# Fused attention and two-layer kernel: first weight chunks unpacked in PSUM, keys of units 0 to 3 by TensorE transposes, low half of g on VectorE in 16 steps

## The chip, the cores and the metric

The kernel runs on one core of a Trainium2 chip. The metric is device time in microseconds (us); lower is better. Engines: TensorE (PE, its weight loads PEld), VectorE (DVE), ScalarE (ACT), GpSimd (POOL), and SyncE (SP), which issues the DMAs.

## The reference, cut

```python
# attention with decay: 4 batches, 8 heads, 768 tokens, head size 48
for t in range(S):
    y[:, :, t] = einsum('bhd,bhde->bhe', r_t, state + (u * k_t) v_t)
    state = w * state + k_t v_t
x = y as (3072, 384)
# first layer: 384 -> 2048 -> 384
h = x @ w_in
g = h if h >= 1, 0 if h <= -1, else (h + 1)**2 / 4
x1 = g @ w_out
# second layer: each token goes to its best of 8 experts
out = gate * (relu(x1 @ w1[e]) @ w2[e])
```

All tensors are float32. `w_in` and `w_out` arrive as 64-bit numbers.

## The kernel before

Every float32 product is made of three matmuls in a rounded format (`prod3`, lines 293 to 295): high by high, high by low, low by high. So every operand is split into a high half (a ScalarE copy) and a low half (operand minus high half).

**Attention** works on 24 units of 128 tokens, six per batch. For a unit: the transposed r and k are scaled by powers of w (`prep_rk`, VectorE); `s0_pe` multiplies them into two 128x512 products in PSUM, which VectorE masks (`s0_ev`); `s2_pe` adds the unit's keys times values to the state; `s1_pe` makes the transposed output y; `s3_hi` and `s3_lo` split it into `xh` and `xl`. The keys in natural layout (`kk`) are loaded apart and scaled on GpSimd (`prep_kk`). The diagonal term with u is a product on GpSimd (`prep_dv`) that TensorE adds to y by transposes in the first 8 units (`DIAG`); later it is written into the masked product by predicated copies on VectorE (`s0_dg`). The states of units 0 to 4 of the first batch go through an identity matmul (`by_pe`).

**Weights** of the first layer come in 16 chunks of 768 64-bit numbers per partition (`w_load`). Three VectorE passes (`w_bits`, lines 361, 364, 367) put each number's bits together as a float32 in a scratch tile, ScalarE copies the high half (`w_hi`, line 382), GpSimd subtracts (`w_lo`, line 386).

**The first layer** runs in 96 steps, each one block of 512 tokens and 128 of the 2048 columns. A step is 9 matmuls into a bank of tag `h` (two banks), three ScalarE passes into a tile `a` (lines 677, 681, 684), a max on VectorE (line 687), the high half `gh` on ScalarE (line 691), the low half `gl` on GpSimd (line 696), and 9 matmuls into three accumulator banks. The first 14 steps cover columns of blocks 0 and 1. **The second layer** follows with the weights of the expert that token 0 chose; the branch for other experts does not run here.

**The order** of all this is written out by a planner (`Schedule`) when the kernel is built: each task has an engine, a price (`COST`), a due time (shifted by `SHIFT`), the tasks it waits for, and the buffers it takes. The planner fills each engine's list; on the chip each engine works through its list in order and waits for semaphores. Buffers that matter: four `ld` tiles (attention tiles and weight chunks), two `x1` tiles, three PSUM banks `att`, two `h`, three accumulators. `SP` issues loads in the planned order and waits for a free tile. Before the first output matmul, gaps that the planner sees on TensorE are filled with matmuls that do nothing (`keep_warm`, line 602).

Of the kernel before, what the change touches and what calls it, by code (L numbers as in the profile page):

```python
# [33 lines left out]
DIAG = 8  # L34
# [23 lines left out]
class Schedule:  # L58
# [5 lines left out]
    LOCK = {"rk", "wb1", "wb2", "wb3", "dd", "x2l", "w2lo", "slo"}  # L64
# [150 lines left out]
SHIFT = {"dd": -118.5, "dg": -152.25, "dg2": 85, "dp": -121, "dv": 7, "e0": 37.75, "e0c": -69.5, "e0l": 11.25, "e1":  # L215
# [3 lines left out]
         5.75, "max": -5, "mixl": 6, "o": 18.5, "o2": -773.75, "oh": -43.5, "ost": -52.5, "over": 99.75,  # L219
# [30 lines left out]
def fused_kernel(ctx, tc, att, wcol, wrow, ub, ucol, win, wout, emb, tau, w1, w2, out):  # L250
# [268 lines left out]
    def by_pe(u):  # L519
        return u < UPB - 1  # L520
# [165 lines left out]
    def m1_max(a, hp):  # L686
        nc.vector.tensor_tensor(out=a, in0=hp, in1=a, op=ALU.max)  # L687
# [356 lines left out]
    first = {n: i - 100 for i, n in enumerate("a0 w0 n0 ub b0 a1 n1 b1 w1".split())}  # L1044
# [6 lines left out]
    for u in range(NU):  # L1051
# [13 lines left out]
        l2 = add("l2", f"u{u}", "SP", 1.1, lambda u=u: att_load(u, "n"), due=first.get(f"n{u}", due - 9 - 2), alloc=[nb])  # L1065
        rk = add("rk", f"u{u}", "DVE", 1.57, lambda u=u: prep_rk(u), [l0], due - 8, use=[ab])
        kk = add("kk", f"u{u}", "Pool", 1.3, lambda u=u: prep_kk(u), [l2, wkc], due - 6, alloc=[kkb], use=[nb])
        if u < RAMP:
# [3 lines left out]
            dg = add("dg", f"u{u}", "ACT", 0.2, lambda u=u: dg_ev(u), [dp], due - 5.4, alloc=[dgb], use=[dpb])  # L1072
# [4 lines left out]
        if u < DIAG:  # L1077
# [39 lines left out]
    for ci, c in enumerate([x for f in range(NF // 2) for x in (("in", f), ("out", f))]):  # L1117
# [443 lines left out]
```

## Time and profile before

| | |
|---|---|
| median of 3 runs | 739.37 us (738.45 to 743.44) |
| profiled execution | 740.02 us, span 738.1 us |
| TensorE busy | 721.9 us (98%), 4977 matmuls |
| VectorE, ScalarE, GpSimd busy | 381.7, 394.0, 280.1 us |
| DMA | 73.45 MB |

The span runs from the first to the last instruction. An engine is busy while an instruction of its own executes; TensorE's filler matmuls count as busy.

### The profile page before, as it was taken

To read this page: it belongs to the slowest core of one execution; us is meant where nothing else is said; L and a number is where in the kernel's file an instruction comes from. 1 tells how busy PE (TensorE), PEld (TensorE's weight loads), DVE (VectorE), ACT (ScalarE), POOL (GpSimd) and SP (SyncE) were. 2 spreads that over 40 slices of the span, in tenths; PEclk is the share of its full clock that TensorE was granted. 3 is DMA by queue.
4 is the path that set the end of the run, shared out by engine and by line. 5 is a ranking of instruction groups with operands and counts; after the bars stand their busy time and mean duration, and the time that the engine had idled before them with its cause. 6 is when DMAs were issued, how large, how long until landed. Compare 5 with 4: busy or idle time off the path is not lost.

```text
span 738.1 us, 12336 instructions
## 1 busy us (share of the span) xinstructions
PE 721.9 (98%) x4977; PEld 596.5 (81%) x4977; DVE 381.7 (52%) x606; ACT 394.0 (53%) x700; POOL 280.1 (38%) x225
## 2 busy tenths in 40 slices
PE   8899999999999999999999999999999999999995
PEld 6777887777888877887888888887989898879994
DVE  7789799787871363367455452132233324142342
ACT  2365758654656377566775676666243324252343
POOL 6899986845535254234423142333010100100000
PEclk9999999999999999999999999999999999999999
DMA  7746444434330253134353142001111202001100
GB/s 265 271 170 238 148 170 138 137 126 130 134 136 1 66 185 130 40 132 149 129 170 129 44 130 85 1 0 44 44 43 44 86 1 85 11 12 44 65 22 27
DMA packets 24724, 73.45 MB, mean 100 GB/s; under 512 B 2377, under 2 KB 8658, under 8 KB 24658
## 3 DMA queue, kind: packets, MB, share of 16 engines
q1 hardware_dynamic: 24658, 72.57, 29.3%
q8 instruction: 41, 0.67, 0.4%
q14 instruction: 25, 0.20, 0.1%
HBM read 61.56 MB, written 11.01 MB: 98 GB/s over the span
## 4 chain that ended last, share of the span: by engine, by line
PE 87%; DVE 4%; DMA 4%; ACT 2%; issue 1%; POOL 0%; SPq 0%; ACTq 0%; POOLq 0%; DVEq 0%
PE psh L293 13%; PE psh L294 12%; PE psh L295 12%; PE acc L293 9%; PE acc L294 9%; PE acc L295 9%; PE o L295 5%; PE o L293 4%; PE o L294 4%; PE psy L535 4%; DMA att<-att 3%; PE psa L502 3%; PE pskv L564 1%; DMA w<-win 1%; DVE sc L367 1%
## 5 line engine op out<-in xcount | busy, mean ns | idle before, releaser
L696 POOL TENSOR_TENSOR gl<-a,gh 128x512 fp32r<-128x512 f32 x96 | 137.9, 1447 | 183.8 <-ACT gh L691 180.0
L687 DVE TENSOR_TENSOR a<-psh,a 128x512 f32<-128x512 f32 x96 | 66.1, 689 | 134.8 <-ACT a L684 126.2
L293 PE MATMUL psh<-xh,win_h 128*128 128x512 f32 x288 | 115.9, 402 | 1.0 <-DVE a L687 0.9
L293 PE MATMUL acc<-gh,wout_h 128*128 128x512 f32 x288 | 114.8, 399 | 0.0
L294 PE MATMUL acc<-gl,wout_h 128*128 128x512 f32 x288 | 113.9, 396 | 0.0
L295 PE MATMUL acc<-gh,wout_l 128*128 128x512 f32 x288 | 113.9, 395 | 0.0
L294 PE MATMUL psh<-xl,win_h 128*128 128x512 f32 x288 | 113.8, 395 | 0.0
L295 PE MATMUL psh<-xh,win_l 128*128 128x512 f32 x288 | 113.8, 395 | 0.0
L677 ACT ACTIVATE a<-psh,half 128x512 f32<-128x512 f32 x96 | 65.7, 684 | 74.9 <-PE psh L295 60.4
L954 ACT ACTIVATE gh<-psh 128x512 fp32r<-128x512 f32 (+1 forms) x56 | 30.0, 536 | 108.7 <-PE psh L295 107.0
L959 DVE SCALAR_TENSOR_TENSOR gl<-psh,gh 128x512 fp32r<-128x512 f32 (+1 forms) x56 | 34.4, 614 | 102.8 <-ACT gh L954 102.7
L831 POOL TENSOR_TENSOR sq<-sq 128x512 f32<-128x512 f32 (+1 forms) x14 | 15.9, 1135 | 182.4 <-ACT sq L826 161.1
L691 ACT ACTIVATE gh<-a 128x512 fp32r<-128x512 f32 x96 | 59.4, 624 | 32.0 <-DVE a L687 19.2
L293 PEld LDWEIGHTS psh<-xh,win_h 128*128 128x128 f32 x288 | 54.1, 188 | 16.9 <-DVE a L687 2.3
L295 PE MATMUL o<-w2h,gl 128*128 128x384 f32 x192 | 65.0, 339 | 1.4 <-DVE gl L959 1.4
L293 PEld LDWEIGHTS acc<-gh,wout_h 128*128 128x128 f32 x288 | 54.1, 188 | 13.7 <-issue 0.4
L293 PE MATMUL o<-w2h,gh 128*128 128x384 f32 x192 | 64.8, 337 | 0.1
L295 PEld LDWEIGHTS psh<-xh,win_l 128*128 128x128 f32 x288 | 54.1, 188 | 13.1
L294 PEld LDWEIGHTS acc<-gl,wout_h 128*128 128x128 f32 x288 | 54.1, 188 | 13.0 <-POOL gl L696 0.4
L295 PEld LDWEIGHTS acc<-gh,wout_l 128*128 128x128 f32 x288 | 54.1, 188 | 13.0
L294 PE MATMUL o<-w2l,gh 128*128 128x384 f32 x192 | 64.5, 336 | 0.0
L294 PEld LDWEIGHTS psh<-xl,win_h 128*128 128x128 f32 x288 | 54.1, 188 | 12.2
(167 smaller groups left out, 1290.1 us busy)
## 6 DMA issues: line engine op xcount, KB each, us to landing
att<-att SPq DMA_DIRECT2D x22, 736.0 KB, 5.3
w<-wout SPq DMA_DIRECT2D x16, 768.0 KB, 4.2
w<-win SPq DMA_DIRECT2D x16, 768.0 KB, 4.3
attn<-att SPq DMA_DIRECT2D x20, 384.0 KB, 4.2
x1d<-x SPq DMA_DIRECT2D x6, 768.0 KB, 4.1
out<-o SPq DMA_DIRECT2D x11, 384.0 KB, 2.5
x1f<-x1d SPq DMA_DIRECT2D x5, 768.0 KB, 4.9
hw<-w SPq DMA_DIRECT2D x8, 384.0 KB, 3.8
```

The source lines that it names most:

```text
L293: nc.tensor.matmul(o, lhsT=sh, rhs=mh, start=first, stop=False, skip_group_check=True)
L294: nc.tensor.matmul(o, lhsT=sh, rhs=ml, start=False, stop=False, skip_group_check=True)
L295: nc.tensor.matmul(o, lhsT=sl, rhs=mh, start=False, stop=last, skip_group_check=True)
L502: nc.tensor.matmul(a[j][:, p, :], lhsT=s["k2"][64 * j:64 * j + 64, p, :], rhs=s["r2"][64 * j:64 * j + 64, p, :], start=True, stop=True)
L535: nc.tensor.matmul(o, lhsT=lhsT, rhs=rhs, start=q in fresh, stop=stop, skip_group_check=True)
L677: nc.scalar.activation(out=a, in_=hp, func=AF.Relu, bias=half[:, 0:1], scale=0.5)
L687: nc.vector.tensor_tensor(out=a, in0=hp, in1=a, op=ALU.max)
L691: nc.scalar.activation(out=gh, in_=a, func=AF.Copy)
L696: (eng or nc.gpsimd).tensor_tensor(out=gl, in0=a, in1=gh.bitcast(F32), op=ALU.subtract)
L831: nc.gpsimd.tensor_tensor(out=q[:, 0, :n], in0=q[:, 0, :n], in1=q[:, kk, :n], op=ALU.add)
L954: nc.scalar.activation(out=gh, in_=hp, func=AF.Relu)
L959: nc.vector.scalar_tensor_tensor(out=gl, in0=hp, scalar=0.0, in1=gh.bitcast(F32), op0=ALU.max, op1=ALU.subtract)
```

## The change

Constants choose how many units or steps take a new path.

- `KK_PE` 4: units 0 to 3 get their natural keys from `kk_pe`, four TensorE transposes of the scaled keys into a bank `att`, and `kk_ev`, a ScalarE copy. Their loads in natural layout are gone.
- `W_PSUM` 2: chunks 0 and 1 land in the two `x1` tiles. Their bits are put together in two accumulator banks (`w_pbits`), and `w_psplit` makes the high half on ScalarE and the low half on VectorE.
- `G_PSUM` 16: in steps 0 to 15 the max writes into the `h` bank; ScalarE and VectorE take the high and the low half from there. The bank is held until then, and `a` only until the max.
- `DV_PSUM` 4: in units 0 to 3 `prep_dv` runs on VectorE and reads its small factor from PSUM; the copy `dg_ev` is gone there.
- `DIAG` is 6 in place of 8, `BY_PE` is 4 in place of 5.
- The loads are asked for in the order a0, b0, a1, b1, w0, w1, `SHIFT` is another table, and the planner prices the routing steps `rt3` higher. `ON_DVE` is empty.

```diff
-DIAG = 8
+DIAG = 6
 ...
     if kind == "rt3":
-        return 0.12 if eng == "ACT" else {0.3: 0.35, 0.9: 0.95, 1.0: 1.1}[dur]
+        return 1.45 if eng == "ACT" else {0.3: 0.37, 0.9: 1.25, 1.0: 1.3}[dur]
 ...
+KK_PE, W_PSUM, G_PSUM, DV_PSUM, BY_PE = 4, 2, 16, 4, 4
 ...
     def w_load(c):
         kind, f = c
-        t = atp.tile([128, 1536], F32, tag="ld", name="w64", bufs=4).bitcast(U64)
+        if 2 * f + (kind == "out") < W_PSUM and c not in stage_t:
+            t = xp.tile([128, KD, 512], F32, tag="x1", name="w64").rearrange("p k n -> p (k n)").bitcast(U64)
+        else:
+            t = atp.tile([128, 1536], F32, tag="ld", name="w64", bufs=4).bitcast(U64)
 ...
+    def w_pbits(c, i):
+        t64 = stage_t[c]
+        hw, lw = t64[:, :, 1], t64[:, :, 0]
+        if i == 1:
+            w_buf[c] = [psum(f"acc{j + 1}", [128, 512], "psw", 1)[:, :x.stop - x.start] for j, x in w_parts(c)]
+        for j, x in w_parts(c):
+            m = w_buf[c][j].bitcast(U32)
+            if i == 1:
+                nc.vector.tensor_scalar(out=m, in0=hw[:, x], scalar1=3, scalar2=0x3FFFFFFF, op0=ALU.logical_shift_left,
+                                        op1=ALU.bitwise_and)
+            elif i == 2:
+                nc.vector.scalar_tensor_tensor(out=m, in0=hw[:, x], scalar=0xC0000000, in1=m, op0=ALU.bitwise_and,
+                                               op1=ALU.bitwise_or)
+            else:
+                nc.vector.scalar_tensor_tensor(out=m, in0=lw[:, x], scalar=29, in1=m, op0=ALU.logical_shift_right,
+                                               op1=ALU.bitwise_or)
 ...
+    def w_psplit(c, lo):
 ...
+            if lo:
+                nc.vector.tensor_tensor(out=l, in0=m, in1=h.bitcast(F32), op=ALU.subtract)
+            else:
+                nc.scalar.activation(out=h, in_=m, func=AF.Copy)
 ...
+    def kk_pe(u):
+        st[u]["kkp"] = psum("att", [128, NP, C], "pskk", 3)
+        for p in range(NP):
+            nc.tensor.transpose(st[u]["kkp"][:, p, :], st[u]["k2"][:, p, :], ident)
+
+    def kk_ev(u):
+        st[u]["kk"] = atp.tile([128, H, D], F32, tag="kk", name="kk", bufs=2)
+        nc.scalar.activation(out=st[u]["kk"].rearrange("q (p j) d -> q p j d", p=NP),
+                             in_=st[u].pop("kkp").rearrange("q p (j d) -> q p j d", j=2)[:, :, :, 0:D], func=AF.Copy)
 ...
-        dg = s["dg"].rearrange("p (a j) -> p a j", a=NP)
+        eng = nc.vector if u < DV_PSUM else elem("dv", f"u{u}")
+        dg = (s["dgp"] if u < DV_PSUM else s["dg"]).rearrange("p (a j) -> p a j", a=NP)
 ...
     def by_pe(u):
-        return u < UPB - 1
+        return u < BY_PE
 ...
-    first = {n: i - 100 for i, n in enumerate("a0 w0 n0 ub b0 a1 n1 b1 w1".split())}
+    first = {n: i - 100 for i, n in enumerate("a0 b0 a1 b1 w0 w1".split())}
 ...
-        l2 = add("l2", f"u{u}", "SP", 1.1, lambda u=u: att_load(u, "n"), due=first.get(f"n{u}", due - 9 - 2), alloc=[nb])
+        l2 = u >= KK_PE and add("l2", f"u{u}", "SP", 1.1, lambda u=u: att_load(u, "n"), due=first.get(f"n{u}", due - 9 - 2), alloc=[nb])
 ...
-        wb, sb = Buf("ld"), Buf("x1")
+        wb, sb = Buf("x1" if ci < W_PSUM else "ld"), Buf("x1")
 ...
+        gk = "h" if k < G_PSUM else "a"
+        gb = hb if k < G_PSUM else ab
+        q = add("max", f"k{k}", "DVE", 0.7, lambda k=k, gk=gk: m1_max(got["a", k], got["h", k], got[gk, k]), [q], T[k], use=[ab, hb])
+        q = add("gh", f"k{k}", "ACT", 0.65, lambda k=k, n=n, gk=gk: got.update({("gh", k): m1_gh(got[gk, k], n)}), [q], T[k], alloc=[ghb], use=[gb])
+
+        def gl(k=k, s=s, gk=gk):
+            gq[s[:3]] = got["gh", k], m1_gl(got[gk, k], got["gh", k], s[3], nc.vector if k < G_PSUM else elem("gl", f"k{k}"))
+        q = add(*(("glp", f"k{k}", "DVE") if k < G_PSUM else ("gl", f"k{k}", "Pool")), 1.45, gl, [q], T[k], alloc=[glb], use=[gb, ghb])
```

## Rows read from the trace of the kernel before

**Rows 1.** Stretches of the span: length, busy us (instructions) of each engine, clock, DMA.

```profile
0.00:7.11 7.11, 4.79 (x25) 4.49 (x25) 4.22 (x15) 1.77 (x2) 2.44 (x14) 1.00 0.59 186
7.11:38.93 31.82, 28.76 (x444) 22.60 (x444) 25.41 (x28) 9.25 (x27) 27.05 (x24) 1.00 0.83 289
38.93:160.00 121.07, 120.76 (x843) 96.66 (x840) 107.11 (x108) 80.66 (x138) 98.60 (x65) 1.00 0.49 166
...
730.82:738.10 7.28, 0.00 (x0) 0.00 (x0) 0.42 (x1) 0.45 (x2) 0.00 (x0) 0.86 0.21 66
sum 738.10, PE 721.89 PEld 596.53 DVE 381.71 ACT 394.01 POOL 280.12; mean PE 72.19 PEld 59.65 DVE 38.17 ACT 39.40 POOL 28.01
```

**Rows 2.** The same view for the filler matmuls of line 602 alone.

```profile
7.11:38.93 31.82, 4.61 (x30) 3.74 (x30) 1.00 0.83 289
38.93:160.00 121.07, 0.71 (x4) 0.52 (x4) 1.00 0.49 166
```

**Rows 3.** Chain that ended last, first 40 us: start, us, what.

```profile
by line: DMA att<-att 37.1%; PE psa L502 9.0%; PE psy L535 6.9%; DVE att L445 6.9%; issue 5.5%; DVE sc L367 4.9%; PE pskv L560 4.0%; POOL kr L464 3.2%; DVE at L510 3.0%; PE psdg L470 2.6%; ACT state L525 2.6%; PE pskv L564 2.5%; PE psy L539
...
15.73 1.20 DVE at L510 x2
16.93 1.96 DVE sc L367
...
18.90 4.73 DMA att<-att
...
28.70 6.36 DMA att<-att
...
35.15 1.24 DVE att L445
```

**Rows 4.** VectorE groups of the first 160 us: busy us, mean ns, idle before.

```profile
L687 DVE TENSOR_TENSOR a<-psh,a 128x512 f32<-128x512 f32 x25 | 17.1, 686 | 10.4 <-ACT a L684 9.8 <-POOL ru L459 0.3
...
L515 DVE COPY_PREDICATED at<-ident,dg 128x512 f32<-128x512 int32 x4 | 5.7, 1479 | 0.0
L595 DVE TENSOR_TENSOR xl<-psy,xh 128x384 fp32r<-128x384 f32 x9 | 4.9, 549 | 0.4 <-ACT xh L589 0.2
```

**Rows 5.** One line, the second unpack pass: shortest, median, longest in ns.

```profile
L364 DVE SCALAR_TENSOR_TENSOR sc<-w,sc x16: 957/1654/2526, 12.0 to 144.4; 128x768 uint32<-128x768 uint32 x16
```

**Rows 6.** TensorE in order of time: start, us, what; first 75 us.

```profile
5.85 0.66 PE L608 MATMUL pstw<-ident,pwt 128*128 128x128 f32 x4
6.34 0.39 PE L602 MATMUL wu<-mask,ident 128*128 128x128 f32 x2
...
37.59 0.91 PE L560 MATMUL pskv<-state,ident 128*128 128x384 f32 x2
38.44 0.56 PE L564 MATMUL pskv<-att,kk 128*48 128x48 f32 x16
...
62.85 0.49 PE L539 MATMUL psy<-ident,dv 128*128 128x128 f32 x3
63.27 1.08 PE L535 MATMUL psy<-at,att 128*32 128x128 f32 x32
```

**Rows 7.** GpSimd groups of the first 160 us: busy us, mean ns, idle before.

```profile
L696 POOL TENSOR_TENSOR gl<-a,gh 128x512 fp32r<-128x512 f32 x24 | 40.1, 1676 | 15.0 <-ACT gh L691 11.1 <-issue 3.6 <-PE psh L295 0.2
L386 POOL TENSOR_TENSOR win_l<-sc,win_h 128x768 fp32r<-128x768 f32 x8 | 16.4, 2053 | 3.8 <-ACT win_h L382 3.7
```

**Rows 8.** Waits of TensorE: total us, times, longest.

```profile
PE o L295 <- DVE gl L959: 1.4, 2, 0.7
```

**Rows 9.** All engines in order of time, 82.3 to 89 us.

```profile
82.33 0.39 PE L293 MATMUL psh<-xh,win_h 128*128 128x512 f32 x1
...
86.08 0.63 ACT L684 ACTIVATE a<-a 128x512 f32<-128x512 f32 x1
...
86.82 0.69 DVE L687 TENSOR_TENSOR a<-psh,a 128x512 f32<-128x512 f32 x1 [3.30 <-ACT a L684]
...
88.63 0.40 PE L293 MATMUL psh<-xh,win_h 128*128 128x512 f32 x1
```

More of the change, by code (lines that the diff above doesn't have):

```diff
@@ L63 @@
             "PE": {"ACT": 0.24, "DVE": 0.2, "Pool": 0.25}, "Pool": {"ACT": 0.09, "DVE": 0.09, "PE": 0.12}}
-    LOCK = {"rk", "wb1", "wb2", "wb3", "dd", "x2l", "w2lo", "slo"}
+    LOCK = {"rk", "wb1", "wb2", "wb3", "dd", "x2l", "w2lo", "slo", "krv", "kkv", "dvv", "ru0v", "ru1v", "wlov", "glv"}
     MAIN = {"h", "o", "h2", "o2", "rt0"}
@@ L72, in add @@
         due += self.shift.get(kind, 0) + self.shift.get(item, 0)
+        if eng == "Pool" and (kind, item) in ON_DVE:
+            kind, eng = kind + "v", "DVE"
         t = Task(kind, item, eng, cost(kind, item, eng, dur), fn, deps, due, list(alloc), list(use) + list(alloc), list(after))
@@ L171 @@
         "t5a": 0.12, "tw": 0.85, "dp": 0.84, "t4": 0.2, "pe0": 0.2, "pe1": 0.25, "le1": 0.1, "fl1": 0.1, "rt2": 0.2,
[1 row of a table removed]
+        "s0": 0.89, "krv": 0.605, "kkv": 0.475, "dvv": 0.55, "ru0v": 0.475, "ru1v": 0.475, "wlov": 0.87, "glv": 0.605,
+        "kkt": 0.5, "kkc": 0.42, "dvp": 0.6, "wp1": 0.6, "wp2": 0.93, "wp3": 0.93, "whp": 0.8, "wlp": 0.93, "glp": 0.605}
 COST_256 = {"x2h": 0.33, "sqa": 0.33, "shi": 0.33, "x2l": 0.34, "slo": 0.34, "gl2": 0.34, "gh2": 0.31, "rt1": 0.31,
@@ L212, in d_pe @@
     return n / 2300 + 0.011
-SHIFT = {"dd": -118.5, "dg": -152.25, "dg2": 85, "dp": -121, "dv": 7, "e0": 37.75, "e0c": -69.5, "e0l": 11.25, "e1":
[3 rows of a table removed]
-         5.75, "max": -5, "mixl": 6, "o": 18.5, "o2": -773.75, "oh": -43.5, "ost": -52.5, "over": 99.75,
[26 rows of a table removed]
+SHIFT = {"": 368.5, "b0": 11, "b1": 72.75, "b2": 141.5, "b3": -2.5, "b4": -265.5, "b5": -0.25, "b6": 172.25, "dd":
[28 rows of a table added]
+         "whi": -44.75, "whp": 130, "wkc": 32.5, "wl": 7.75, "wlo": -99.25, "wlp": -90.5, "wp1": -36, "wp2": 14.75,
+         "wp3": 40.5, "x1ld": -15.75, "x1st": -1, "x2l": -19.25, "x2ld": -68}
 U_DVE, U_PE, W_DVE = 4.7, 3.5, 4.0
+ON_DVE = {}
+KK_PE, W_PSUM, G_PSUM, DV_PSUM, BY_PE = 4, 2, 16, 4, 4
 @with_exitstack
@@ L369, in w_bits, with w_parts @@
             del stage_t[c]
+    def w_parts(c):
+        n = 256 if c[0] == "in" else 384
+        return [(0, slice(0, n)), (1, slice(n, 768))]
+    def w_pbits(c, i):
[14 more added lines that the diff above has]
+                                               op1=ALU.bitwise_or)
+        if i == 3:
+            del stage_t[c]
+    def w_psplit(c, lo):
+        kind, f = c
+        for j, x in w_parts(c):
+            if kind == "in":
+                sl = (slice(None), slice(x.start // 256, x.stop // 256), slice(2 * f * 128, (2 * f + 2) * 128))
+                h, l = win_h[sl], win_l[sl]
+                m = w_buf[c][j].rearrange("p (k f) -> p k f", f=256)
+            else:
+                sl = (slice(None), 2 * f + j)
+                h, l, m = wout_h[sl], wout_l[sl], w_buf[c][j]
+            if lo:
+                nc.vector.tensor_tensor(out=l, in0=m, in1=h.bitcast(F32), op=ALU.subtract)
+            else:
+                nc.scalar.activation(out=h, in_=m, func=AF.Copy)
     def w_views(c):
@@ L382, in w_hi, with w_lo @@
         nc.scalar.activation(out=h, in_=m, func=AF.Copy)
-    def w_lo(c, eng):
+    def w_lo(c, eng=None):
+        eng = eng or elem("wlo", "w%d" % (2 * c[1] + (c[0] == "out")))
         h, l, m = w_views(c)
@@ L446, in prep_rk, with elem @@
         st[u].update(zip(("r2", "k2"), att_views(u)))
+    def elem(kind, u):
+        return nc.vector if (kind, u) in ON_DVE else nc.gpsimd
     def prep_kk(u):
@@ L450, in prep_kk @@
         st[u]["kk"] = atp.tile([128, H, D], F32, tag="kk", name="kk", bufs=2)
-        nc.gpsimd.tensor_tensor(out=st[u]["kk"], in0=t[:, 0:DM].rearrange("p (h d) -> p h d", h=H), in1=wk, op=ALU.mult)
+        elem("kk", f"u{u}").tensor_tensor(out=st[u]["kk"], in0=t[:, 0:DM].rearrange("p (h d) -> p h d", h=H), in1=wk, op=ALU.mult)
+    def kk_pe(u):
[6 more added lines that the diff above has]
+                             in_=st[u].pop("kkp").rearrange("q p (j d) -> q p j d", j=2)[:, :, :, 0:D], func=AF.Copy)
     def prep_ru(u, i):
@@ L456, in prep_ru @@
             st[u]["ru"] = atp.tile([128, NP, C], F32, tag="ru", name="ru").rearrange("p a t -> p (a t)")[:, 0:DM]
-            nc.gpsimd.tensor_tensor(out=st[u]["ru"], in0=t[:, 0:DM], in1=ubt, op=ALU.mult)
+            elem("ru0", f"u{u}").tensor_tensor(out=st[u]["ru"], in0=t[:, 0:DM], in1=ubt, op=ALU.mult)
         else:
-            nc.gpsimd.tensor_tensor(out=st[u]["ru"], in0=st[u]["ru"], in1=t[:, DM:2 * DM], op=ALU.mult)
+            elem("ru1", f"u{u}").tensor_tensor(out=st[u]["ru"], in0=st[u]["ru"], in1=t[:, DM:2 * DM], op=ALU.mult)
     def prep_kr(u):
@@ L463, in prep_kr @@
         s["kr"] = atp.tile([128, NP, C], F32, tag="ru", name="kr")
-        nc.gpsimd.tensor_tensor(out=s["kr"], in0=s["k2"], in1=s["r2"], op=ALU.mult)
+        elem("kr", f"u{u}").tensor_tensor(out=s["kr"], in0=s["k2"], in1=s["r2"], op=ALU.mult)
     def dg_pe(u):
@@ L494, in prep_dv @@
             dst = s["dv"][:, o:o + 8 * n].rearrange("p (a j x) -> p a j x", a=NP, j=2)
-            nc.gpsimd.tensor_tensor(out=dst, in0=src, in1=bcast(dg.unsqueeze(3), [128, NP, 2, n]), op=ALU.mult)
+            eng.tensor_tensor(out=dst, in0=src, in1=bcast(dg.unsqueeze(3), [128, NP, 2, n]), op=ALU.mult)
     def s0_pe(u):
@@ L684, in m1_sq, with m1_max @@
         nc.scalar.activation(out=a, in_=a, func=AF.Square, bias=1.0, scale=-1.0)
-    def m1_max(a, hp):
-        nc.vector.tensor_tensor(out=a, in0=hp, in1=a, op=ALU.max)
+    def m1_max(a, hp, out=None):
+        nc.vector.tensor_tensor(out=a if out is None else out, in0=hp, in1=a, op=ALU.max)
     def m1_gh(a, n):
@@ L1064, in fused_kernel @@
             l0 = l1 = add("l01", f"u{u}", "SP", 2.1, lambda u=u: att_load(u, "av"), due=due - 8 - 2, alloc=[ab])
-        l2 = add("l2", f"u{u}", "SP", 1.1, lambda u=u: att_load(u, "n"), due=first.get(f"n{u}", due - 9 - 2), alloc=[nb])
+        l2 = u >= KK_PE and add("l2", f"u{u}", "SP", 1.1, lambda u=u: att_load(u, "n"), due=first.get(f"n{u}", due - 9 - 2), alloc=[nb])
         rk = add("rk", f"u{u}", "DVE", 1.57, lambda u=u: prep_rk(u), [l0], due - 8, use=[ab])
-        kk = add("kk", f"u{u}", "Pool", 1.3, lambda u=u: prep_kk(u), [l2, wkc], due - 6, alloc=[kkb], use=[nb])
+        if u < KK_PE:
+            ktb = Buf("att")
+            kk = add("kkt", f"u{u}", "PE", 0, lambda u=u: kk_pe(u), [rk], due - 6, alloc=[ktb, kkb], use=[ab])
+            kk = add("kkc", f"u{u}", "ACT", 0, lambda u=u: kk_ev(u), [kk], due - 6, use=[ktb, kkb])
+        else:
+            kk = add("kk", f"u{u}", "Pool", 1.3, lambda u=u: prep_kk(u), [l2, wkc], due - 6, alloc=[kkb], use=[nb])
         if u < RAMP:
@@ L1071, in fused_kernel @@
             dp = add("dp", f"u{u}", "PE", 0.65, lambda u=u: dg_pe(u), [kr], due - 5.5, alloc=[dpb], use=[rub])
-            dg = add("dg", f"u{u}", "ACT", 0.2, lambda u=u: dg_ev(u), [dp], due - 5.4, alloc=[dgb], use=[dpb])
+            dg = dp if u < DV_PSUM else add("dg", f"u{u}", "ACT", 0.2, lambda u=u: dg_ev(u), [dp], due - 5.4, alloc=[dgb], use=[dpb])
         else:
@@ L1076, in fused_kernel @@
             dg = add("dg2", f"u{u}", "DVE", 0.56, lambda u=u: prep_dg(u), [ru1], due - 4.5, alloc=[dgb], use=[rub])
-        if u < DIAG:
+        if u < DV_PSUM:
+            dv = add("dvp", f"u{u}", "DVE", 0, lambda u=u: prep_dv(u), [dp, l1], due - 4.5, alloc=[dvb], use=[ab, dpb])
+        elif u < DIAG:
             dv = add("dv", f"u{u}", "Pool", 2.0, lambda u=u: prep_dv(u), [dg, l1], due - 4.5, alloc=[dvb], use=[ab, dgb])
@@ L1120, in fused_kernel @@
         due = T[k] - 6 + (4 if kind == "out" else 0)
-        wb, sb = Buf("ld"), Buf("x1")
+        wb, sb = Buf("x1" if ci < W_PSUM else "ld"), Buf("x1")
         wl = add("wl", f"w{ci}", "SP", 2.19, lambda c=c: w_load(c), due=first.get(f"w{ci}", due - 10 - 2), alloc=[wb])
         p = wl
+        if ci < W_PSUM:
+            pb = [Buf("acc1"), Buf("acc2")]
+            for i in range(1, 4):
+                p = add(f"wp{i}", f"w{ci}", "DVE", 0, lambda c=c, i=i: w_pbits(c, i), [p], due - 6 + i * 0.8,
+                        alloc=pb if i == 1 else [], use=[wb] + (pb if i > 1 else []))
+            p = add("whp", f"w{ci}", "ACT", 0, lambda c=c: w_psplit(c, False), [p], due - 2, use=pb)
+            w_ready[c] = add("wlp", f"w{ci}", "DVE", 0, lambda c=c: w_psplit(c, True), [p], due, use=pb)
+            continue
         for i in range(1, 4):
@@ L1127, in fused_kernel @@
         p = add("whi", f"w{ci}", "ACT", 0.84, lambda c=c: w_hi(c), [p], due - 2, use=[sb])
-        p = add("wlo", f"w{ci}", "Pool", 2.1, lambda c=c: w_lo(c, nc.gpsimd), [p], due, use=[sb])
+        p = add("wlo", f"w{ci}", "Pool", 2.1, lambda c=c: w_lo(c), [p], due, use=[sb])
         w_ready[c] = p
```

5 lines of the change are left out of this document (removed), and 58 rows, old and new, of tables (COST, SHIFT).

## The prediction

> **What bounds the kernel now.** I read the table of stretches first, because it says where TensorE is not at work [rows 1]. It is busy for 721.89 of the 738.10 us span, at a granted clock of 1.00 in each stretch in which it works. The 16.21 us that it idles are 2.32 before 7.11 us, 3.06 from there to 38.93, 0.31 up to 160, and 7.28 after its last matmul, while the stores finish; 3.24 are left for the 570 us between 160 and 730.82. Busy isn't useful: the filler matmuls that keep the engine warm take 4.61 us between 7.11 and 38.93, and 0.71 after that [rows 2]. So nearly everything that can be won without removing matmuls is in the 32 us ahead of the first product of the first layer: 3.06 + 4.61 = 7.67 us there, and 0.31 + 0.71 + 3.24 = 4.26 us later. 11.9 us is the ceiling.
>
> The chain that ended last says why the first stretch is loose [rows 3]. Of the first 40 us, 37% of the chain is the load of an attention tile. The third unpack pass of a weight chunk ends at 18.90 us; at that instant the load of unit 3 starts, since the chunk held one of four `ld` buffers. It lands at 23.63. The load of unit 4 starts at 28.70, again when a buffer comes free, and its multiply can begin at 35.15. So buffers set when loads start, and loads set when units start. VectorE and GpSimd are busy for 25.41 and 27.05 of the 31.82 us [rows 1], but they are behind the loads here.
>
> After 38.93 TensorE is dense, with VectorE at 107.11 of 121.07 us and GpSimd at 98.60. There a change of engine is worth nothing by itself; it can only cost.
>
> **The change, part by part.** The sum is made against the profiled execution, 740.02 us (its span and 1.92 outside it); the median of the runs shown is 0.65 lower.
>
> **Loads.** Units 0 to 3 keep the four `ld` buffers to themselves and chunks 0 and 1 go to the two `x1` buffers; the four natural-layout loads of units 0 to 3 disappear from SP's queue, and where the two chunks stand among units 2 and 3 is left to the due times. Four tiles of 736 KB and two chunks of 768 KB are 4.59 MB. By 7.11 us the old kernel had moved 186 x 7.11 = 1.32 MB, and then moved 289 GB/s [rows 1]; the remaining 3.27 MB take 11.3 us. All six are there by about 18.4 us (an estimate from those two rates), where unit 3 alone came at 23.63. Unit 4 can be fetched when unit 0 is done. Loads leave the path.
>
> **What is late next.** TensorE itself: of the 31.82 us, 31.82 - 7.67 = 24.15 are its own work, and VectorE runs close behind. Per unit VectorE has the multiply (1.24), two maskings (1.20 together) [rows 3], the low half of x (0.55) [rows 4], and now the two small products of `prep_dv`, which have 384 elements in all with one operand in PSUM. The nearest row is again 0.55 for 384; they lie between that and twice that, and I take 0.7. That is 3.7 a unit, 14.8 for four, 1.24 for unit 4, and two chunks. No row has an integer operation into PSUM; a pass lies between the 0.957 that its fastest SBUF twin took [rows 5] and two halves at the price of the 0.55 row, 1.1. Three passes and the low half make 3.8 to 4.4 a chunk, I take 4. The two accumulator banks that hold a chunk meanwhile come back when its low half is done, near 30 us, and the first output matmuls need them only after the first product and its chain of six steps; if that cover were gone it would cost those matmuls the remainder of a chunk, up to 4. In total 24 us of work from about 6 us on, with the same end in view as TensorE. Two engines that are both full don't mesh perfectly; I leave 2.5 of the 7.67 us standing (bounds 0 and 5.5). Gain 5.2.
>
> **Keys by transposes.** Four transposes for each of units 0 to 3. The same four transposes of the table took 0.66 us, with the next matmul 0.49 after their start [rows 6]: 1.96 to 2.64, I take 2.3, all on TensorE's own path. GpSimd loses four multiplies, ScalarE gets four copies (it is busy for only 9.25 of 31.82 us [rows 1], so nothing).
>
> **Units 4, 6 and 7.** With `BY_PE` 4, unit 4's state no longer goes through the identity matmul: 38.44 - 37.59 = 0.85 us less. With `DIAG` 6, the transposed products of units 6 and 7 go: 63.27 - 62.85 = 0.42 each [rows 6]. These lie where TensorE is dense, so 1.7 come off. For it VectorE gets two small state operations and four predicated copies of 1.48 us on average [rows 4]. Net on TensorE with the keys: +0.6 (0.3 to 0.9).
>
> **Low half of g on VectorE for 16 steps.** 16 x 0.69 = 11.0 us [rows 4] go to VectorE, and 16 x 1.68 = 26.8 leave GpSimd [rows 7]. With two chunks' low halves (2 x 2.05) GpSimd loses at least 31 of its 128 us up to 160 us, the keys and six `dv` besides [rows 1, 7]. VectorE gains 11.0, about 2.8 for `dv`, 4 x 1.48 = 5.9, 2.2 for the low halves and at most 1.1 for two state operations smaller than the 0.55 row, less some 2 for four passes that fall from 1.65 to 1.1: about 21. But its passes are stretched where they meet GpSimd: the second pass takes 0.957 at best and 1.654 in the median, in 16 runs [rows 5]; that is 11 us for this line alone. If 31/128 of it goes, with as much on the other two passes together, some 5 us come back. Net +16, with 6.4 + 14.0 = 20.4 us of idle time between 7.11 and 160 [rows 1]. It fits, barely: nothing won and nothing lost, which is where the prediction can break.
>
> **The rest of the schedule.** The table of due times is replaced, so everything is reordered, SP's and GpSimd's queues too. The 4.26 us of late gaps are not tied to a resource that is full; 1.4 of them are two waits for the low half of the second layer [rows 8], which comes after a ScalarE copy; what ScalarE does for routing stands in the same queue, and the planner priced it at 0.12 and now prices it at 1.45. I count 2.5 gained and 1.8 left (bounds 0 and 4.26; new gaps are as easy to make as to close).
>
> **Sum.** 740.02 - 5.2 + 0.6 - 2.5 = 732.9 for the profiled kind of run, and 0.65 less for the median: **732.3 us**. The first product of the first layer should start some 3 us earlier, near 36, if unit 4's products stay ahead of it as now.
>
> **The rivals.** (A) **The start is only re-bound.** Three PSUM banks (`att`) carry five tiles a unit in place of four, and VectorE is full: if 5.5 of the 7.67 us stay, the start gives 2.2, the keys eat 0.6 net, and with anything from nothing to 2.5 us gained later the time is 735.3 to 737.8. For it: VectorE's 25.41 of 31.82 us, and both engines meeting the same end. Against it: the chain names loads, not VectorE.
>
> (B) **The PSUM buffers of the first layer turn too slowly: slower.** The result of max now stays in the `h` bank, which is free only after both halves of g are taken. Take one step [rows 9]: its matmuls start at 82.33, the max ends at 87.51, and the same bank is taken again at 88.63: 1.12 us of slack. The new holding adds a ScalarE copy (0.63, as the square before it), a VectorE pass of 0.69 and two hand-overs like that from the square to the max (86.71 to 86.82), together 1.5. That alone makes TensorE wait 0.4, if no other matmuls are put between, and as it works in order the output matmuls and attention products queued behind wait too; if VectorE is in an unpack pass of 1 to 2.5 us when the low half is due, 1.5 to 2. Ten steps (6 to 15) at 1.2 are 12 us: **744**, between 738 and 752. From about 0.7 us a step it takes more than the 7.1 us of the forecast. Against it: the buffer `a` comes free earlier, and GpSimd's 1.68 us step falls out of the chain.
>
> Here a rule speaks against the change: the Trainium skill, "PSUM — Partial Sum Buffer", in its summary of rules for kernel authors, says to evacuate promptly because PSUM is small. By that rule the result would be B's, 744; the row's slack of 1.12 us against 1.5 agrees for this step, but not for a step with attention products in between, so the sum keeps 732.3.
>
> (C) **Everything meshes.** Both loose stretches go entirely: 740.02 - 11.9 + 0.6 - 0.65 = 728.0. Against it: the old plan left 11.9 with the same planner.
>
> **How the numbers follow.** The forecast case (729.5 to 735) has 0.57, A 0.18, B 0.13, C 0.12. The range 727.5 to 740.5 takes in C, the forecast and A, and leaves out most of B. About 1% is what a measurement of this kernel tells from no change: 7.4 us, so faster means below 732.0 and slower above 746.8. Faster: half of the forecast case and C, 0.40. Slower: the upper part of B, 0.05. The rest, 0.55, is no change that can be told.
>
> **What would show it.** In the changed profile: loads of all six tiles issued before 8 us, and no attention load on the chain of the first 40 us; the first matmul into the `h` banks near 36 us; at most 2.5 us of filler and idle before it; four-transpose groups of about 0.5 us; TensorE still dense up to 160 us with VectorE above 107 us busy; second-pass median below 1.65. I'm wrong if TensorE waits for VectorE's low half of g or for the `h` banks by more than 3 us in total (B), if filler and idle ahead of the first layer stay above 6 us (A), or if new gaps open after 160 us.

## The result

The changed kernel is slower: 749.46 us (median of 7 runs, 748.68 to 751.56) against 740.13 us, ratio 1.0116 with a 95% interval of 1.0088 to 1.0145. The forecast was 732.3 us, and the time lies outside its range.

The stretches of the profile after (length, busy us and instructions of each engine, clock, DMA share, GB/s), to be read beside [rows 1]. The profiled execution took 751.56 us, its span is 749.8.

```profile
0.00:7.11 7.11, 4.58 (x24) 4.20 (x24) 4.22 (x15) 1.77 (x2) 2.45 (x14) 1.00 0.62 195
7.11:35.76 28.65, 26.47 (x435) 21.25 (x435) 26.96 (x48) 10.64 (x31) 14.03 (x10) 1.00 0.79 288
35.76:147.90 112.14, 109.47 (x731) 85.27 (x730) 98.66 (x123) 72.98 (x125) 59.01 (x41) 1.00 0.52 174
147.90:155.40 7.50, 5.23 (x17) 3.92 (x16) 2.29 (x7) 5.08 (x9) 2.68 (x3) 0.77 0.00 0
155.40:178.10 22.70, 22.70 (x294) 17.76 (x292) 13.11 (x24) 12.91 (x26) 10.75 (x10) 1.00 0.32 109
178.10:189.90 11.80, 6.24 (x33) 4.72 (x32) 8.17 (x12) 4.99 (x8) 1.28 (x1) 0.71 0.77 287
189.90:260.00 70.10, 68.38 (x523) 53.93 (x524) 43.74 (x68) 42.03 (x72) 29.97 (x25) 1.00 0.48 168
260.00:741.95 481.95, 481.56 (x2910) 404.15 (x2908) 175.46 (x346) 243.90 (x433) 111.17 (x89) 1.00 0.16 53
741.95:749.80 7.85, 0.00 (x0) 0.00 (x0) 0.93 (x4) 0.35 (x1) 0.00 (x0) 0.74 0.19 62
```

The first layer starts at 35.76 us where it started at 38.93, so the start is 3.17 us shorter, as forecast. In the profiles of the runs below it starts between 35.4 and 36.9 us, so the gain there is 2.0 to 3.5 us. Everything is lost behind it: two stretches, from 147.9 and from 178.1 us, hold 2.27 and 5.56 us of idle TensorE, and the granted clock falls to a mean of 0.77 and 0.71 there. From the first layer to the last matmul TensorE now idles 2.67 + 2.27 + 5.56 + 1.72 + 0.39 = 12.6 us, where it idled 0.31 + 3.24 = 3.5 [rows 1].

Waits of TensorE after (total us, times, longest), the two that matter:

```profile
PE psh L298 <- DVE a L748: 9.7, 5, 5.6
PE psh L298 <- DVE gl L757: 2.6, 4, 0.9
```

A wait "for a" is a first layer that needs an `h` bank which VectorE's max has not yet read. What the max was late for stands in the order of time. First the wait of 5.56 us: SyncE's queue, then VectorE, then TensorE (start, us, engine and line, what, idle before it).

```profile
141.21 0.33 SPq L348 DMA_DIRECT2D w<-win  x1
164.81 0.33 SPq L348 DMA_DIRECT2D w<-wout  x1
171.85 0.59 SPq L792 DMA_DIRECT2D x1p<-x1d  x1
172.49 0.60 SPq L336 DMA_DIRECT2D att<-att  x1
```

```profile
163.84 0.94 DVE L357 TENSOR_REDUCE least<-w 128x1 f32<-128x768 f32 x1
...
170.87 0.95 DVE L357 TENSOR_REDUCE least<-w 128x1 f32<-128x768 f32 x1
180.03 1.23 DVE L492 TENSOR_TENSOR att<-att,pwt 128x1024 f32<-128x1024 f32 x1 [8.21 <-DMA att<-att]
181.29 0.56 DVE L656 TENSOR_TENSOR xl<-psy,xh 128x384 fp32r<-128x384 f32 x1
181.76 1.28 DVE L571 TENSOR_TENSOR at<-psa,mask 128x512 f32<-128x512 f32 x2
182.96 0.68 DVE L748 TENSOR_TENSOR a<-psh,a 128x512 f32<-128x512 f32 x1
```

```profile
177.74 0.39 PE L300 MATMUL acc<-gh,wout_l 128*128 128x512 f32 x1
183.69 0.79 PE L298 MATMUL psh<-xh,win_h 128*128 128x512 f32 x1 [5.56 <-DVE a L748]
```

Line 348 loads a weight chunk again, late in the kernel, only to look for values that are too small (ScalarE's Abs, then line 357). Chunk 0 is loaded at 141.21 us, chunk 1 at 164.81, as soon as line 357 has read chunk 0. The reload of half of block 1 (line 792) goes out at 171.85, as soon as line 357 has read chunk 1 (170.87 + 0.95). The attention load stands behind it in SyncE's queue, goes out at 172.49 among five others, and lands near 180. VectorE stands still for 8.21 us with that unit's multiply (line 492) at the head of its queue; the max of a step of the first layer, whose last ScalarE pass ended at 176.03, is queued behind it.

The cause of that chain is in two lines. `w_load` takes an `x1` tile for the first chunks if `c not in stage_t`; `w_look` and the unpack delete the entry, so the condition is true again for the second load. The planner puts all sixteen look loads into `ld` buffers (`wb = Buf("ld")`); on the chip the first two share the two `x1` tiles with block 1's reload. In the kernel before, chunk 0 was loaded for this only at 252.04 us; the new due times put it at 141.21, ahead of that reload.

The wait of 2.27 us, VectorE and then ScalarE after:

```profile
139.41 1.98 DVE L679 TENSOR_SCALAR wrc<-mix 1x384 f32<-1x384 f32 x1 [0.37 <-POOL gl L757]
141.43 1.53 DVE L681 TENSOR_TENSOR wrc<-wrc,mix 1x384 f32<-1x384 f32 x1
...
144.20 0.54 DVE L690 TENSOR_REDUCE ess<-esq 8x1 f32<-8x384 f32 x1
...
149.69 1.29 DVE L748 TENSOR_TENSOR a<-psh,a 128x512 f32<-128x512 f32 x2 [1.19 <-ACT a L745]
```

```profile
144.84 0.69 ACT L738 ACTIVATE a<-psh,half 128x512 f32<-128x512 f32 x1 [4.40 <-DVE ess L690]
```

The tables of the routing (clamped weights, squared embeddings) are made in the two `a` tiles through which every step's relu, square and max pass. They hold both from 139.4 to 144.7 us, so ScalarE's next relu waits 4.40 us, and the chain to the max ends late by what TensorE then waits. In the kernel before they held the same tiles 20 us later, from 159.20 us, where ScalarE's relu waited 3.3 us and TensorE, in among attention products, idled 1.22 us of the 18 from 160 to 178, 0.45 of it for the max. These two tiles are in the plan (`tb`), unlike those of the look loads; but the plan prices the first two passes over the clamped weights at 0.9 us each, and they took 1.98 and 1.53.

### The profile page after: what moved, and what is told of

The parts are those of the page before. It is cut to its first block, busy times and chain, and to the rows that moved or that the text cites. A ratio compares the mean times of both kernels' runs of the same rounds, so it can differ in the third digit from the quotient of the medians.

```text
span 749.8 us, 12288 instructions
## 1 busy us (share of the span) xinstructions
PE 724.6 (97%) x4957; PEld 595.2 (79%) x4957; DVE 373.5 (50%) x646; ACT 394.6 (53%) x702; POOL 231.3 (31%) x191
## 4 chain that ended last, share of the span: by engine, by line
PE 76%; ACT 7%; DVE 6%; DMA 5%; issue 3%; POOL 1%; SPq 0%; ACTq 0%; DVEq 0%
PE psh L298 12%; PE psh L299 11%; PE psh L300 11%; PE acc L298 7%; PE acc L299 6%; PE acc L300 6%; PE o L298 4%; PE o L300 4%; PE o L299 4%; PE psy L596 3%; PE psa L563 2%; DMA w<-win 2%; DMA att<-att 2%; ACT a L738 2%; ACT a L742 1%
## 5 line engine op out<-in xcount | busy, mean ns | idle before, releaser
L757 POOL TENSOR_TENSOR gl<-a,gh 128x512 fp32r<-128x512 f32 x80 | 107.7, 1350 | 210.4 <-ACT gh L752 210.4
L298 PE MATMUL psh<-xh,win_h 128*128 128x512 f32 x288 | 118.3, 411 | 12.5 <-DVE a L748 9.7
L748 DVE TENSOR_TENSOR a<-psh,a 128x512 f32<-128x512 f32 x80 | 54.9, 690 | 138.1 <-ACT a L745 137.8
L752 ACT ACTIVATE gh<-a 128x512 fp32r<-128x512 f32 x80 | 49.8, 625 | 36.9 <-PE acc L300 27.6
L299 PEld LDWEIGHTS psh<-xl,win_h 128*128 128x128 f32 x288 | 55.0, 191 | 12.4 <-DVE xl L656 0.5
```

Source lines behind the costliest of these rows:

```text
L298: nc.tensor.matmul(o, lhsT=sh, rhs=mh, start=first, stop=False, skip_group_check=True)
L299: nc.tensor.matmul(o, lhsT=sh, rhs=ml, start=False, stop=False, skip_group_check=True)
L748: nc.vector.tensor_tensor(out=a if out is None else out, in0=hp, in1=a, op=ALU.max)
L752: nc.scalar.activation(out=gh, in_=a, func=AF.Copy)
L757: (eng or nc.gpsimd).tensor_tensor(out=gl, in0=a, in1=gh.bitcast(F32), op=ALU.subtract)
```

## The experiments

Each starts from the changed kernel unless it says otherwise, and keeps the order of instructions on every engine. The ratio is to the kernel before, which was run again beside each (medians of 739.47 to 740.14 us there).

| kernel | us, median | ratio, 95% interval |
|---|---|---|
| changed kernel | 749.46 | 1.0116, 1.0088 to 1.0145 |
| e1_look_ld | 741.95 | 1.0023, 0.9997 to 1.0048 |
| e2_tab_mix | 744.54 | 1.0068, 1.0047 to 1.0089 |
| e3_look_and_tab | 738.59 | 0.9979, 0.9961 to 0.9996 |
| e4_g_sbuf | 753.45 | 1.0191, 1.0138 to 1.0243 |
| e6_late_look | 742.32 | 1.0034, 1.0012 to 1.0055 |
| e9_gl_pool | 745.30 | 1.0065, 1.0047 to 1.0083 |
| e10_fill | 752.33 | 1.0151, 1.0118 to 1.0184 |
| e12_fill | 750.16 | 1.0134, 1.0109 to 1.0159 |
| e13_fill9 | 746.36 | 1.0096, 1.0072 to 1.0120 |
| e11_warm | 737.20 | 0.9963, 0.9945 to 0.9981 |
| e14_bank | 736.79 | 0.9961, 0.9945 to 0.9977 |

The gains told below are differences of the medians. By the ratios e1 gains 6.9 us, e2 3.6 and e3 10.1.

**e1_look_ld: the tile of the look loads.**

```
-    def w_load(c):
+    def w_load(c, look=False):
-        if 2 * f + (kind == "out") < W_PSUM and c not in stage_t:
+        if 2 * f + (kind == "out") < W_PSUM and not look:
```

> Only the tile changes: the second loads of weight chunks 0 and 1, made to look for small values, go into the 12 KB buffers of the attention loads instead of the x1 tiles; the order on every engine stays. Theory T1 (one x1 tile serialises look load 0, look load 1 and the reload of block 1's first half, and SyncE holds the attention load of 172.49 us behind them): TensorE's 5.56 us wait at 178 us falls below 2 us, the low clock after it (about 3.5 us) goes too, and the time is 740 to 743 us. Rival T2 (sixteen look loads that now come between 141 and 270 us crowd the queue and the buffers, whichever buffers they use): the wait stays above 4 us, time 747 to 751 us.

Measured: 741.95 us, 7.5 less. SyncE's queue in this run, to be held against the four rows of the changed kernel:

```profile
155.88 0.33 SPq L348 DMA_DIRECT2D w<-win  x1
162.51 0.33 SPq L348 DMA_DIRECT2D w<-wout  x1
162.94 0.98 SPq L792 DMA_DIRECT2D x1p<-x1d  x1
165.79 0.33 SPq L336 DMA_DIRECT2D att<-att  x1
```

The reload goes out 8.91 us earlier and the attention load 6.70, though look load 0 itself goes later. The largest wait that is left near there is 0.34 us. T1 holds.

**e6_late_look: the look loads held back** (the planner is run a second time with every other engine order fixed; the sixteen loads may not start before 380, 383, ... us of its plan; the first two keep their `x1` tiles).

```
+    for task in sch.again(dict(zip([t for t in sch.tasks if t.kind == "lkl"], range(380, 428, 3)))):
```

> The sixteen look loads with their ScalarE and VectorE steps are held back to between 380 and 428 us of the plan; every other instruction keeps its order on its engine. T1 and T2 together (the looks are the cause, by their tile or by their number): the waits of TensorE at 150 us (partly), 178, 220 and 256 us shrink to under 1 us each, time 737 to 742 us. Rival T3 (the tables' use of the two 'a' tiles and GpSimd's share with VectorE cause the gaps): the wait at 150 us stays at 2 us or more, and the time stays above 746 us.

Measured: 742.32 us, the same as e1 within the intervals. So where the sixteen loads stand (T2) costs nothing that can be told once the first two don't hold the `x1` tiles that block 1 needs; sixteen more transfers between 141 and 270 us are hidden. The wait at 150 us is unchanged at 2.29 us in both, which speaks for T3 as a second cause.

**e2_tab_mix: the tables' temporaries.**

```
-    mix = atp.tile([64, DM], F32, name="mix")
+    mix = atp.tile([128, DM], F32, name="mix")
-            r["wrc"] = tmp512("wrc")[32:33, 0:DM]
+            r["wrc"] = mix[64:65, :]
-            r["esq"] = tmp512("esq")[0:E, 0:DM]
+            r["esq"] = mix[96:96 + E, :]
-            r['zer'] = tmp512('zer')[:, 0:KD * NL]
+            r['zer'] = atp.tile([128, KD * NL], F32, name='zer')
```

> The three temporaries of the tables (clamped weights, squared embeddings, zeros) get places of their own and no longer use the two 'a' tiles that a step's max and g pass through; the order stays. T3: the 2.27 us wait at 150 us goes to under 0.7 us and the low clock of the 5 us behind it goes, time 744.5 to 746 us. Rival: ScalarE's relu waits for the same VectorE and table work in its queue anyway; the wait at 150 us stays within 0.5 us, time 748.5 to 751 us.

Measured: 744.54 us, 4.9 less, the best that was expected. TensorE is busy for all 15.00 us from 145 to 160; the wait of 5.7 us for the attention load stays.

**e3_look_and_tab: the edits of e1 and e2 together.**

> Both mends at once: look loads 0 and 1 in the attention buffers and the tables' temporaries in places of their own; same order. If the two waits (5.56 us at 178, 2.27 us at 150, each with its stretch of low clock) are separate and are the whole loss against the kernel before, the gains of the single mends add (7.5 and 4.9 of 749.5): 736 to 738.5 us, faster than the kernel before by 1 to 4 us. Rival: one mend only lets the other wait grow or a third takes its place: 740 to 742 us.

Measured: 738.59 us, 10.9 less than the changed kernel where the sum of the two was 12.4; faster than the kernel before by 0.2%. That is just above the 736 to 738.5 expected, and the rival (740 to 742) is out. The two conflicts, with the low clock behind them, are the whole loss and a little more. Its stretches, the first ending at its first layer:

```profile
7.11:35.59 28.48, 26.84 (x437) 21.36 (x436) 27.57 (x49) 11.13 (x32) 14.23 (x10) 1.00 0.79 292
35.59:160.00 124.41, 122.47 (x895) 96.01 (x895) 106.51 (x143) 84.48 (x143) 66.60 (x47) 1.00 0.46 157
160.00:726.70 566.70, 565.78 (x3606) 471.12 (x3605) 234.13 (x439) 297.83 (x527) 150.03 (x121) 1.00 0.22 76
```

This profiled execution took 736.03 us, the lowest of its twelve. In six of the ten profiles that have the new start without extra fillers the granted clock falls between 12 and 20 us (0.79 to 0.84); in this one it doesn't. e11_warm, below, looks into that.

**e4_g_sbuf: rival B undone.** In steps 0 to 15 max, gh and gl go through the SBUF tile `a` again; gl stays on VectorE.

```
-        q = add("max", ..., lambda k=k, gk=gk: m1_max(got["a", k], got["h", k], got[gk, k]), ...)
+        q = add("max", ..., lambda k=k: m1_max(got["a", k], got["h", k], got["a", k]), ...)
```

> In steps 0 to 15 max, gh and the low half of g go through the SBUF tile 'a' again, so that the PSUM bank of h is free after max; the subtraction stays on VectorE and the order stays. Rival B of the prediction (the bank is held too long): the four waits of 0.50 to 0.87 us at 95.7 to 111.3 us go, time about 746 to 747.5 us, since only 2.6 us of 9.3 are theirs. Other theory (VectorE's queue is what is late, whatever the buffer): the waits move to the 'a' tile, 748.5 to 751 us.

Measured: 753.45 us, 4.0 more. Both expectations missed. The waits of the first layer for gl are gone, but two output matmuls wait 0.64 each for it, and the tile takes over: a first layer now waits 1.93 us for the max at 124.08, with a mean clock of 0.57 from 125 to 129, and one for the low half of x 1.32 at 71.75. From the first layer behind the wait at 124.08 to the next one takes 1.64 us longer than the same in e3, so part of the 4.0 is the clock's. In this order, held in the bank, g is the cheaper way.

**e9_gl_pool: gl of steps 0 to 15 back on GpSimd,** on top of e3, with max, gh and gl in `a` as in e4.

```
-    ... m1_gl(got[gk, k], got["gh", k], s[3], nc.vector if k < G_PSUM else elem("gl", f"k{k}"))
+    ... m1_gl(got["a", k], got["gh", k], s[3], elem("gl", f"k{k}"))
```

> On top of both mends the low half of g of steps 0 to 15 goes back from VectorE to GpSimd, read from the SBUF tile 'a' as in the kernel before; the order of the instructions stays. Theory (VectorE is 99% busy from 20 to 40 us and the sixteen subtractions cost it 16 x 0.69 = 11 us): gl leaves VectorE, the late-queue waits at 95 to 111 us go, time 735 to 737. Rival (a GpSimd subtraction takes 1.8 us and stretches VectorE's passes meanwhile, and the output matmuls then wait for gl): slower than e3_look_and_tab by 2 to 8 us.

Measured: 745.30 us, 6.7 more than e3. Waits of TensorE in this run:

```profile
PE psh L298 <- DVE a L748: 3.8, 6, 1.7
...
PE acc L299 <- POOL gl L757: 3.3, 3, 1.1
```

The rival holds: the output matmuls wait for GpSimd. Part of the 6.7 is the tile's, as in e4 (4.0), and no run parts the two; together, gl on VectorE from the bank is better than what it replaced.

**e10_fill, e12_fill, e13_fill9: the price of the clock.** Extra matmuls, their results unused, in the places where TensorE waits. e10 put 9 ahead of step 23 and 22 ahead of step 29, e12 the 22 ahead of step 28, e13 the 9 alone.

```
+        if (task.kind, task.item) == ("h", "k23"):
+            fill = psum("att", [128, 512], "fill", 3)
+            for _ in range(9):
+                nc.tensor.matmul(fill, lhsT=win_h[:, 0, 0:128], rhs=win_h[:, 0, 0:512], start=True, stop=True)
```

> The changed kernel as it is, with 9 extra matmuls of 512 columns ahead of step 23's first layer and 22 ahead of step 29's, where TensorE sat idle for 2.27 and 5.56 us; what they compute is not used. The waits stay; only TensorE's idleness in them is filled. If the low granted clock behind each wait (0.87 and 0.54; 0.89 and 0.55) is a cost of its own, it stays at 1.00 there and the time falls by the 2.6 and 3.5 us that I read from the slower matmuls: 743.5 to 746 us. If the slow matmuls only delay work that waits for other engines anyway, 748.5 to 751 us.

> e10_fill with its second set of 22 matmuls ahead of step 28's first layer, where the wait is (ahead of step 29's they were 5.2 us of added work). The first set of e10_fill kept the granted clock at 1.00 behind the wait at 150 us. If the low clock behind a wait is a cost of its own, it now stays at 1.00 behind both, and the time is 744 to 747 us although both waits are as long as before; if other engines set the pace there, 748.5 to 751 us.

> The changed kernel with the first set of fillers alone: 9 matmuls of 512 columns (9 x 0.235 = 2.1 us) in the 2.27 us in which TensorE waited ahead of step 23. By e10_fill, less its 22 misplaced matmuls (5.2 us), the low clock behind that wait costs 2.3 us: 746.5 to 748 us. If what ran slowly there was only waiting for others: 748.8 to 750.5 us.

Measured: 752.33, 750.16 and 746.36 us. The stretch behind the first wait, in the changed kernel and in e13:

```profile
150.00:155.00 5.00, 4.57 (x13) 3.64 (x14) 1.41 (x5) 2.67 (x5) 2.68 (x3) 0.67 0.00 0
```

```profile
150.00:155.00 5.00, 5.00 (x50) 3.92 (x53) 1.42 (x5) 3.65 (x7) 2.70 (x3) 1.00 0.00 0
```

With the wait filled the clock stays at 1.00, and TensorE's next first layer is held up as long. The median is 3.1 us lower, but the two intervals overlap (by the ratios it is 1.5), and 0.76 us stand in the second wait, which is 4.80 in that profile instead of 5.56. What the clock cost is better read from rows. e3 has the same order of matmuls, and TensorE is busy throughout from the first layer of step 23 to that of step 25, and from step 28 to step 29. The changed kernel, then e3:

```profile
150.43:158.05 7.62, 7.62 (x75) 5.92 (x75) 1.68 (x5) 4.71 (x8) 2.90 (x4) 0.78 0.01 3
183.69:192.03 8.34, 8.34 (x40) 6.45 (x41) 6.43 (x17) 5.10 (x8) 1.28 (x1) 0.66 0.65 225
```

```profile
146.86:152.82 5.96, 5.96 (x76) 4.67 (x74) 1.13 (x4) 3.65 (x7) 2.39 (x4) 1.00 0.02 4
172.82:178.63 5.81, 5.81 (x42) 4.57 (x41) 4.90 (x10) 4.04 (x7) 1.34 (x2) 1.00 0.73 262
```

So the stretch behind the first wait is 1.66 us longer and that behind the second 2.53, 4.2 in all, where e10's expectation read 2.6 and 3.5. In e13 the first of them takes 6.05 us, so nearly all of the 1.66 is the clock's. But it takes 6.06 in e1, whose wait is as long and not filled: the clock stayed at 1.00 there too. So that the filling kept the clock up is likely, not shown. The second wait was filled in no run: in e10 the 22 matmuls stood behind it as plain work (22 x 0.234 = 5.2 us), and in e12 they waited 3.79 us themselves for a PSUM bank of `att` that line 656 was to free.

**e11_warm: e3 with fillers in the start.**

```
+        if task.kind == "s2" and task.item in ("u1", "u3"):
+            keep_warm(5)
```

> e3_look_and_tab with five more 128-column fillers of TensorE ahead of the state matmuls of units 1 and 3, where it sat idle for 0.56 to 1.11 and for 1.05 us in the first 30 us. Theory: the runs of the new start in which the granted clock falls to about 0.8 between 12 and 20 us do so because of these gaps (50 fillers of before are now 20 to 26), and that is what lifts the median of e3_look_and_tab (738.6) above its profiled run (736.0): the clock stays at 1.00 there and the median falls to 736 to 737.5 us. Rival: VectorE, 99% busy up to 40 us, sets the first layer's start whatever TensorE's clock, or the fillers delay the state matmuls: median 738 to 740 us.

Measured: 737.20 us. From 12 to 20 us, e2_tab_mix (one of those with the low clock) and e11_warm:

```profile
12.00:20.00 8.00, 6.89 (x84) 5.07 (x83) 7.61 (x15) 3.60 (x11) 2.27 (x2) 0.79 1.03 398
```

```profile
12.00:20.00 8.00, 8.00 (x150) 6.70 (x149) 7.69 (x15) 3.52 (x11) 2.28 (x2) 1.00 1.01 391
```

The median is 1.4 us lower than e3's; the two intervals overlap, so that it is the fillers is not settled. The clock is at 1.00 in both profiles that have them, but so it is in four of the ten without. Its price there is small: the first layer starts at 36.16 us in e11, and between 36.2 and 36.9 in the six profiles with the low clock (35.6 to 36.5 in the other four).

**e14_bank: e11 with steps 10 to 12 through `a`.**

```
+        gk = "a" if k in (10, 11, 12) else gk
```

> e11_warm with max, gh and gl of steps 10, 11 and 12 in the SBUF tile 'a' instead of the PSUM bank, every other step and the order as before; these are the steps whose late gl held the bank for which the first layers of steps 12 to 14 waited 0.50 to 0.63 us each at 95 to 106 us. Rival B at its place: the three waits (1.8 us) go and nothing takes their place, since the tile is asked for again only after the next first layer, 2.1 us later: 735 to 736.3 us. Other theory (as in e4_g_sbuf, a step's relu then waits for the tile): 737 to 739 us.

Measured: 736.79 us, 0.4 below e11 and not to be told from it; the 735 to 736.3 of rival B missed. The three waits for gl became one of 1.07 us at 108.61, at the step behind them, the first whose bank is again held for gl.

## Why the prediction was wrong, step by step

**Loads** and **what is late next** were right in the main. All six loads leave SyncE's queue by 5.73 us, and chunk 1, the last asked for, lands near 18.1 (18.4 forecast). The attention loads left the chain, the loads did not: the first 40 us are led by the load of a weight chunk (21.7%) where an attention tile's had 37.1% [rows 3]. VectorE is busy for 26.96 of 28.65 us. What stays ahead of the first layer is 28.65 - 26.47 = 2.18 us of idle time and 0.94 of filler, 3.1 against 2.5 forecast: 4.55 gained instead of 5.2. Rival A is out. In e3's profile the gain is still there at the end: the first layer of step 0 starts 3.3 us before that of the kernel before, the last one 4.3.

**Keys and units 4, 6 and 7.** The sixteen transposes take 2.6 us (2.3 forecast), the transposed products fall from 4.3 to 3.1, the identity matmuls of the state from 4.3 to 3.6: net +0.7 against +0.6.

**Low half of g.** 16 passes of 0.679 us against 0.69. The second unpack pass fell from a median of 1.654 [rows 5] to 0.959, but its longest is 2.525 still, and that is where rival B happens.

**Rival B** was right as a mechanism and wrong in size. VectorE, then GpSimd after, at the first of the four waits (TensorE goes on at 95.73):

```profile
92.55 2.52 DVE L372 SCALAR_TENSOR_TENSOR sc<-w,sc 128x768 uint32<-128x768 uint32 x1
95.00 0.68 DVE L757 TENSOR_TENSOR gl<-psh,gh 128x512 fp32r<-128x512 f32 x1
```

```profile
92.41 1.85 POOL L433 TENSOR_TENSOR wout_l<-sc,wout_h 128x768 fp32r<-128x768 f32 x1 [3.83 <-ACT wout_h L428]
```

The low half stands behind a stretched pass, the bank behind the low half. But only four steps of the ten are hit, by 0.50 to 0.87 us: 2.6 us, where I priced ten at 1.2; in e3 it is three steps and 1.8 us. The rule that I weighed against the row (the Trainium skill, "PSUM — Partial Sum Buffer", summary of rules for kernel authors: evacuate promptly) would have cost more here: e4 evacuates to SBUF and is 4.0 us slower, as the waits move to the two `a` tiles. The measurement decides.

**The rest of the schedule** is the step that failed. I counted 2.5 us gained there, "bounds 0 and 4.26": the lower bound left out a loss, though the sentence said that new gaps are as easy to make as to close. Between first layer and last matmul the idle time grew by 12.6 - 3.5 = 9.1 us, and the slower matmuls behind two of the new waits took 4.2 more. I had taken the new due times for a shuffle of gaps, and had not followed what they move: the tables, which take both `a` tiles, and the look loads, which by the condition in `w_load` take `x1` tiles. The condition and the new due times stood in the diff, the tables' tiles in the kernel's code. The two waits of 1.4 us that I named [rows 8] did go. With both conflicts mended (e3) the idle time between first layer and last matmul is 1.94 + 0.92 = 2.9 us where idle and filler were 4.26: 1.4 gained of the 2.5, and 1.8 of what is left are rival B's three waits. Whether the plan's low prices put the tables where they did harm, no run tests.

**The sum with what was measured:** 740.02 - 4.55 + 0.7 - 0.71 (fillers behind the first layer) + 9.1 + 0.6 (after the last matmul, 7.85 against 7.28) = 745.2 us, and the profiled execution, the slowest of its seven, took 751.56. Of the 6.4 us between, 4.2 are the matmuls at the low clock, by the rows above; 2.2 stay without a place. No rival had a term for the clock. The same sum for e3 (4.73 gained at the start, 0.69 less idle time behind it, 0.3 more after the last matmul) gives 734.9 against the 736.03 of its profile, the fastest of its twelve. Its median of 738.59 stays 6.3 above the forecast of 732.3: without the two conflicts the change gains 1.0 to 1.6 us, not the 7.1 forecast.

## What to carry to other kernels

Where a planner orders the work, check for each step that is moved, or whose helper is changed, that the buffer which the code takes is the one which the plan counts, for the second call of the helper as well as for the first; two loads in the wrong tiles, ahead of others in an in-order queue, cost 7.5 us. Price a new order on both sides of zero, and a wait of TensorE at more than its length: here 2.27 and 5.56 us of waiting brought 1.66 and 2.53 of slower matmuls. And ask which of two places is scarcer before results are moved out of PSUM early.

## What was not expected of the hardware

- A wait of TensorE may lower its granted clock or not: behind 2.27 us it fell to 0.67 (mean of 150 to 155 us) in the changed kernel, and behind the same wait of 2.29 us it stayed at 1.00 in e1 and e6. Behind 5.56 us the matmuls began slowly at once, with a mean of 0.50 from 183.69 to 189 us, the lower of its two levels; e2, e4, e10 and e13, with 4.80 to 5.71 us of the same wait, show 0.50 to 0.59 in the 3.6 to 5.1 us behind it. The Trainium skill, "TensorE: Matmul & The Clock Gate", section "HAM oscillation — how this bites in real kernels", describes matmuls that start at the low clock after a wait for a transfer; the second wait, which goes back to an attention load, agrees with it.
- From 12 to 20 us the clock was 0.79 to 0.84 in six of ten profiles and 1.00 in four, and TensorE's idle time there does not tell them apart: 0.88 to 1.40 us in the six, 0.56 to 1.36 in the four.
- The second unpack pass takes 0.94 us alone and 2.52 us while GpSimd subtracts in SBUF beside it (92.41 to 94.26 us in the changed kernel); it ends 0.81 us after GpSimd's subtraction. VectorE's subtraction with one operand in PSUM takes 0.68 to 0.69 in all 16 steps of e3, four of them wholly beside a GpSimd instruction.
